# An index load moved behind the columns, and the first gate and up matmuls in a new order, in a kernel that TensorE bounds

## The chip, the cores and the metric

The kernel runs on one core of one Trainium2 chip. The metric is the device time of one execution in microseconds (us). Every run named here is "fast" (no more than 1.5% above the fastest run of its kernel). TensorE is the matmul engine, VectorE and ScalarE are the two elementwise engines, and a load is "landed" when its semaphore says so to the engine that waits.

In the profile lines PE is TensorE, PEld its weight loads, DVE VectorE, ACT ScalarE, POOL GpSimd, SP SyncE (which issues the loads here). L502 is line 502 of the kernel. Times in a view count from the start of the span, which is about 1.7 us shorter than the device time.

## The reference, cut to what matters

```python
def reference(A_x, A_w_r, A_w_i, B_x, B_w_gate, B_w_up, B_w_down):
    x = A_x                                   # (1, 2048, 512) bf16
    xn = _layernorm(x, axis=-1)
    # _A_ref: rfft2 of xn, times (w_r + 1j * w_i), irfft2
    # _B_ref: (gelu(xn @ w_gate) * (xn @ w_up)) @ w_down,  inner size 1792
    return x + _A_ref(xn, A_w_r, A_w_i) + _B_ref(xn, B_w_gate, B_w_up, B_w_down)
```

The change touches only the first microseconds of the second branch: the first rows of `xn`, and the first gate and up projections.

## The kernel before: the parts concerned

The rows are read in 16 "columns" of 128 rows (row 16p + c goes to partition p of column c). Columns 0 and 1 come first; then the index table for gathers much later; then the weights of the gate (`Wg_sb`) and of the up projection (`Wu_sb`), each in two halves: contraction blocks 0 and 1, then 2 and 3.

```python
    pin(load_x(0, 1))
    pin(load_x(1, 1))
    idx_t = pc.tile([P, 3], I32, name="idx_t")
    nc.sync.dma_start(out=idx_t[:], in_=nc.inline_tensor(idx_np, name="spec_rows").ap())
    for T in (Wg_sb, Wu_sb):
        for e in range(0, NE, 2):
            load_w(T, 0, 1024, e=slice(e, e + 2))     # a first or a second half
        if T is Wg_sb:
            load_x(2, 2)                              # columns 2 and 3
    # ... (cut: further columns, weights, constants)
```

The instruction streams of all engines come from a small planner. It is given operations with keys, assumed durations and assumed landing times, and writes down an order; the chip then runs each engine's stream in that order. Units 0 to 3 are the first four pieces of the projections: column 0 and then column 1, each with output blocks 0 to 3 and 4 to 7. Each unit takes 16 gate matmuls and 16 up matmuls of 128 columns, half of them on a first half of the weights.

```python
        T(0, 0)                                  # PE: transposes of column 0
        T(0, 1)
        add("PE", 0.28, spin_on, ...)            # 5 matmuls that only keep TensorE busy
        table = add("ACT", 1.3, lambda: None, [o["root", 1]], key=-1500, lat=1.3)
        # ... (cut)
        o["t", 0] = add("PE", 0.12, lambda: f_T(1, 0, 2), [o["xn1"]], key=1000.13, ...)   # transposes of column 1
        o["t", 1] = add("PE", 0.12, lambda: f_T(1, 2, 2), [o["xn1"]], key=1000.14, ...)
```

## Time and profile before

| before | |
|---|---|
| time, median of the first 3 runs | 178.68 us (178.48 to 178.89) |
| span of the profiled run | 176.9 us |
| TensorE busy | 171.2 us, 97% |
| first gate matmul begins | 6.45 us |
| first up matmul begins | 10.46 us |
| first gate matmul of 256 columns begins | 14.48 us |

The last three rows are moments of TensorE's timeline. They cut the head, that is all up to the first gate matmul of 256 columns, into stretches: what comes before the first useful matmul, the gate matmuls of units 0 to 3, and their up matmuls with the transposes of columns 2 and 3 among them.

### The profile page before, as it was taken

Reading aid. Unit: us, or ns where it says so; the run is one execution under the profiler, and the core shown is the slowest. Engines: PE = TensorE matmul, PEld = TensorE weight load, DVE = VectorE, ACT = ScalarE, POOL = GpSimd, SP = SyncE. Lnnn points to the kernel's source line nnn. Section 1 sums busy time; section 2 is a strip of 40 time slices with the busy share of each in tenths; the row PEclk is TensorE's granted clock in tenths of the full one; section 3 lists DMA queues with packets and bytes.
Section 4 is the critical chain, followed back from the end, with each engine's and each line's share of the span. In section 5 each row is a group of like instructions: output and inputs, shape, how many; then the busy total and the mean of one; then the engine's idle time right before and its main releaser. Section 6 shows DMA issues by size and latency. Waiting matters only on the chain.

```text
span 176.9 us, 3177 instructions
## 1 busy us (share of the span) xinstructions
PE 171.2 (97%) x1158; PEld 96.6 (55%) x1176; DVE 115.6 (65%) x255; ACT 96.4 (55%) x171; POOL 16.7 (9%) x38
## 2 busy tenths in 40 slices
PE   7799999999999999999999999999999999999993
PEld 7699845455545554555555454555445445444463
DVE  3568999988334499969899799843516325345333
ACT  4372489997734998889999973544112111211200
POOL 1020330407750000000000000000000000000000
PEclk9999999999999999999999999999999999999999
DMA  4999997264709602111112312010122222221212
GB/s 100 356 391 382 365 197 115 60 81 106 214 20 310 227 0 59 44 45 33 40 26 60 93 57 59 17 46 0 59 89 89 80 73 67 81 88 60 64 58 59
DMA packets 20847, 19.35 MB, mean 109 GB/s; under 512 B 8480, under 2 KB 17952, under 8 KB 20832
## 3 DMA queue, kind: packets, MB, share of 16 engines
q1 hardware_dynamic: 20416, 17.84, 35.8%
q0 software_dynamic: 416, 1.32, 2.6%
q8 instruction: 9, 0.15, 0.3%
q14 instruction: 6, 0.05, 0.1%
HBM read 13.38 MB, written 2.10 MB: 87 GB/s over the span
## 4 chain that ended last, share of the span: by engine, by line
PE 94%; DMA 2%; issue 1%; SPq 1%; DVE 0%
PE y_ps L833 27%; PE g_ps L494 25%; PE u_ps L494 25%; DMA Wg_sb<-in_B_w_gate_dram 2%; PE g_ps L502 2%; PE yp L784 2%; PE dp L651 2%; PE gp L754 2%; PE u_ps L502 2%; PE bp L593 2%; PE y_ps L837 2%; PE ep L660 2%; SPq L273 0%; PE tp L351 0%; SPq L284 0%
## 5 line engine op out<-in xcount | busy, mean ns | idle before, releaser
L494 PE MATMUL g_ps<-xnT,Wg_sb 128*128 128x512 bf16 (+1 forms) x220 | 52.8, 364 | 0.3
L494 PE MATMUL u_ps<-xnT,Wu_sb 128*128 128x512 bf16 (+1 forms) x216 | 52.5, 364 | 0.3
L833 PE MATMUL y_ps<-Wd_sb,hT 128*128 128x512 bf16 (+2 forms) x246 | 50.8, 355 | 0.3
L512 DVE TENSOR_TENSOR hT<-u_ps,ge 128x512 bf16<-128x512 f32 x56 | 38.4, 688 | 17.2 <-PE u_ps L494 12.4
L507 ACT ACTIVATE ge<-g_ps 128x512 bf16<-128x512 f32 x56 | 33.2, 599 | 21.9 <-PE g_ps L494 19.1
L833 PEld LDWEIGHTS <-hT 128*128 128x128 bf16 x252 | 23.2, 98 | 22.2
L494 PEld LDWEIGHTS <-Wg_sb 128*128 128x128 bf16 x224 | 21.5, 98 | 20.9
L494 PEld LDWEIGHTS <-Wu_sb 128*128 128x128 bf16 x224 | 21.4, 98 | 20.2
L790 ACT CAST yf<-yp 128x512 bf16<-128x512 f32 x16 | 9.3, 586 | 39.4 <-PE yp L784 39.4
L840 DVE TENSOR_TENSOR y_sb<-y_ps,y_sb 128x512 bf16<-128x512 f32 (+2 forms) x18 | 11.1, 631 | 27.9 <-PE y_ps L837 27.9
L665 ACT CAST E<-ep 64x512 bf16<-64x512 f32 x32 | 18.5, 579 | 2.0 <-PE ep L660 1.6
L339 DVE BATCH_NORM_STATS2 stats<-x_t 128x6 f32<-128x512 bf16 x16 | 10.4, 674 | 2.4 <-DMA x_t<-in_A_x_dram 2.4
L456 ACT ACTIVATE xn<-x_t,nb,rstd 128x512 bf16<-128x512 bf16 x12 | 9.4, 807 | 0.6 <-POOL nb L370 0.4
L563 ACT CAST Gs<-gp 128x512 bf16<-128x512 f32 x16 | 8.7, 592 | 1.0 <-PE gp L754 1.0
L563 ACT CAST ds<-dp 128x512 bf16<-128x512 f32 x16 | 8.9, 597 | 0.0
L796 DVE TENSOR_TENSOR lv<-yf 128x512 bf16<-128x512 bf16 x16 | 6.1, 422 | 4.1 <-ACT yf L790 3.2
L563 ACT CAST Bs<-bp 128x512 bf16<-128x512 f32 x16 | 8.3, 601 | 0.5 <-PE bp L593 0.5
L784 PEld LDWEIGHTS <-Gs 128*128 128x128 bf16 x64 | 4.8, 98 | 3.5
L803 DVE TENSOR_TENSOR yt<-lv 128x512 bf16<-128x512 bf16 x16 | 6.1, 422 | 0.3
L784 PE MATMUL yp<-CT,Gs 128*128 128x128 bf16 x64 | 6.0, 220 | 0.1
L837 PE MATMUL y_ps<-yt,RI_t 128*128 128x512 bf16 (+2 forms) x18 | 6.1, 356 | 0.0
L697 DVE TENSOR_TENSOR m<-X,TW 128x1024 bf16<-128x1024 bf16 x8 | 5.5, 688 | 0.2
(67 smaller groups left out, 130.6 us busy)
## 6 DMA issues: line engine op xcount, KB each, us to landing
F<-F SPq DMA_DIRECT2D x32, 64.0 KB, 2.0
y_sb<-in_A_x_dram SPq DMA_DIRECT2D x16, 128.0 KB, 2.1
out_dram<-y_sb SPq DMA_DIRECT2D x15, 128.0 KB, 1.7
x_t<-in_A_x_dram SPq DMA_DIRECT2D x7, 256.0 KB, 8.9
Wd_sb<-in_B_w_down_dram SPq DMA_DIRECT2D x1, 1792.0 KB, 7.5
Wg_sb<-in_B_w_gate_dram SPq DMA_DIRECT2D x2, 512.0 KB, 4.7
Wu_sb<-in_B_w_up_dram SPq DMA_DIRECT2D x2, 512.0 KB, 6.6
Wg_sb<-in_B_w_gate_dram SPq DMA_DIRECT2D x1, 768.0 KB, 9.8
```

The costliest lines, as they stand in the source:

```text
L339: V.bn_stats(out=st[:], in_=x_t[:, c, :])
L456: xn_op[c] = add("ACT", 0.72, lambda c=c: A.activation(out=xn[:, c, :], in_=x_t[:, c, :], func=AF.Identity, bias=nb[:, c:c + 1], scale=rst ...
L494: T_.matmul(b[name][:, f], lhsT=W_[:, e, (f0 + f) * P:(f0 + f + 1) * P], rhs=rhs[:, e, :], start=(e == 0), stop=(e == NE - 1))
L507: A.activation(out=b["ge"][:], in_=b["g_ps"][:], func=AF.Gelu_apprx_tanh)
L512: V.tensor_tensor(out=hT_of(sb, f0, m, o, w), in0=b["u_ps"][:], in1=b["ge"][:], op=ALU.mult)
L563: A.copy(out=o, in_=i)
L665: A.copy(out=b["E"][64 * h:64 * h + 64, r], in_=b["ep", h][64 * r:64 * r + 64])
L784: T_.matmul(t[:, q], lhsT=late["G"][:, q, c0 + j], rhs=IQ[q], start=(q == 0), stop=(q == 3), skip_group_check=True)
L790: A.copy(out=b["yf"][:, j], in_=b[j][:])
L833: T_.matmul(b[o][:], lhsT=hT_of(sb, f, 1, cl * P, P)[:, 0], rhs=Wd_sb[:, f, o:o + w], start=(f == 0), stop=False)
L837: T_.matmul(b[o][:], lhsT=late["RI"][:, c, :], rhs=late["yt"][:, c, o:o + w], start=False, stop=True)
L840: V.tensor_tensor(out=b["y"][:, o:o + w], in0=b[o][:], in1=b["y"][:, o:o + w], op=ALU.add)
```

## The change

Its intent: the weights' issue should follow column 1's at once; TensorE should have work that needs only first halves while second halves are under way, and column 1's transposes should stand early enough to allow that. The rest are new assumed times for the planner, and a small activation that pulls the load of the gelu table forward.

```diff
     pin(load_x(1, 1))
     idx_t = pc.tile([P, 3], I32, name="idx_t")
-    nc.sync.dma_start(out=idx_t[:], in_=nc.inline_tensor(idx_np, name="spec_rows").ap())
     ...
     load_x(14, 2)
+    nc.sync.dma_start(out=idx_t[:], in_=nc.inline_tensor(idx_np, name="spec_rows").ap())
     load_consts("F0", "L0")
     ...
-    LAND = {0: 2.7, 1: 3.4, 2: 7.2, 3: 7.2}
+    LAND = {0: 2.7, 1: 3.4, 2: 7.9, 3: 7.9}
-    WG_LAND = [6.6] * 8 + [13.2] * 6
+    WG_LAND = [7.35] * 8 + [13.2] * 6
     ...
-        table = add("ACT", 1.3, lambda: None, [o["root", 1]], key=-1500, lat=1.3)
+        table = add("ACT", 1.3, lambda: A.activation(out=warm[:], in_=eps_t[:], func=AF.Gelu_apprx_tanh), [o["root", 1]], key=-1500, lat=1.3)
     ...
-        o["t", 0] = add("PE", 0.12, lambda: f_T(1, 0, 2), [o["xn1"]], key=1000.13, lat=0.3, acq=("S",))
-        o["t", 1] = add("PE", 0.12, lambda: f_T(1, 2, 2), [o["xn1"]], key=1000.14, lat=0.3, acq=("S",),
+        o["t", 0] = add("PE", 0.12, lambda: f_T(1, 0, 2), [o["xn1"]], key=1000.01, lat=0.3, acq=("S",))
+        o["t", 1] = add("PE", 0.12, lambda: f_T(1, 2, 2), [o["xn1"]], key=1000.02, lat=0.3, acq=("S",),
     ...  (parts() takes one key for each half)
-            g = parts("g_ps", gt, Wg_sb, 1000 + 0.1 * (k % 2) + 0.4 * (k // 2), (5.3, WG_LAND[0]))
-            u = parts("u_ps", ut, Wu_sb, 1001 + 0.1 * (k % 2) + 0.4 * (k // 2), (8.6, WU_LAND[0]))
+            g = parts("g_ps", gt, Wg_sb, (1000 + (0, 0.03, 0.04, 0.05)[k], 1000.06 + 0.01 * k), (6.0, 7.8))
+            u = parts("u_ps", ut, Wu_sb, (1001 + 0.1 * k, 1001.4 + 0.1 * k), (9.5, 10.85))
```

More of the change, by code (lines that the diff above doesn't have):

```diff
@@ L524, in unit, with parts @@
         if k < 4:
-            def parts(name, tag, W_, key, t):
+            def parts(name, tag, W_, keys, t):
                 o = None
-                for e in (0, 2):
-                    o = add("PE", occ / 2, lambda e=e: mm_part(name, tag, W_, e), [o] if o else [], lat=occ / 2 + 0.3,
-                            key=key + 0.1 * e, acq=() if o else (tag,), t_min=t[e // 2])
-                    o.deps.append(xT_op[c0, 0] if e == 0 else xT_op[c0])
-                    if k == 1 and W_ is Wg_sb:
-                        between["t", 0].deps.append(o) if e == 0 else o.deps.append(between["t", 1])
+                for i, key in enumerate(keys):
+                    o = add("PE", occ / 2, lambda e=2 * i: mm_part(name, tag, W_, e), [o] if o else [], key=key,
+                            lat=occ / 2 + 0.3, acq=() if o else (tag,), t_min=t[i])
+                    o.deps.append(xT_op[c0] if i else xT_op[c0, 0])
+                    if W_ is Wg_sb and i == 0:
+                        if k == 0:
+                            between["t", 0].deps.append(o)
+                        else:
+                            o.deps.append(between["t", 1])
                 return o
             gt = ut = "GU"[k // 2]
-            g = parts("g_ps", gt, Wg_sb, 1000 + 0.1 * (k % 2) + 0.4 * (k // 2), (5.3, WG_LAND[0]))
-            u = parts("u_ps", ut, Wu_sb, 1001 + 0.1 * (k % 2) + 0.4 * (k // 2), (8.6, WU_LAND[0]))
+            g = parts("g_ps", gt, Wg_sb, (1000 + (0, 0.03, 0.04, 0.05)[k], 1000.06 + 0.01 * k), (6.0, 7.8))
+            u = parts("u_ps", ut, Wu_sb, (1001 + 0.1 * k, 1001.4 + 0.1 * k), (9.5, 10.85))
         else:
```

## The prediction

> **What bounds the kernel now.** I read five views in this order: the page (busy times and chain shares), the chain of work in order of time for the first 15 us, the waits of TensorE and of its weight loads, the head in slices of 0.1 us, and the timeline of the head. First the page.
>
> ```profile
> PE 171.2 (97%) x1158; PEld 96.6 (55%) x1176; DVE 115.6 (65%) x255; ACT 96.4 (55%) x171; POOL 16.7 (9%) x38
> ...
> PE 94%; DMA 2%; issue 1%; SPq 1%; DVE 0%
> ```
>
> TensorE is busy for 97% of the span and is 94% of the chain that ended last. The only transfer in that chain is a load of the gate weights, 2%. So there is hardly an engine to relieve: the time is the moment at which TensorE begins its real work, plus its matmuls, plus holes, plus the tail. The chain in order of time shows that moment (columns: start, length, what).
>
> ```profile
> 2.18 4.23 DMA Wg_sb<-in_B_w_gate_dram
> 6.41 0.05 issue
> 6.45 1.07 PE g_ps L502 x16
> 7.52 0.22 PE tp L351 x4
> 7.74 0.03 issue
> 7.77 2.85 PE g_ps L502 x48
> 10.63 1.34 PE u_ps L502 x24
> 11.97 0.45 PE tp L351 x8
> 12.41 2.23 PE u_ps L502 x40
> ```
>
> The first half of the first gate weights (contraction blocks 0 and 1 of four) is issued at 2.18 and lands at 6.41; TensorE starts at 6.45. After 16 matmuls and the 4 transposes of column 1 there is a second piece of "issue" at 7.74. The waits tell what that is (columns: total us, times, longest).
>
> ```profile
> PE sp_ps L320 <- DVE minus_half L266: 1.1, 1, 1.1
> PE g_ps L502 <- DMA Wg_sb<-in_B_w_gate_dram: 0.5, 1, 0.5
> PE tp L351 <- DVE xn L345: 0.4, 1, 0.4
> ...
> PEld L502 <- DMA Wg_sb<-in_B_w_gate_dram: 0.9, 2, 0.7
> ```
>
> These are all of TensorE's listed waits, in the whole run: 2.0 us, all before 6.5 us. Two belong to the gate weights. One is 0.5 us in front of the first matmul. The other shows only in the weight loads: 0.9 in two times, the longest 0.7, so 0.2 us is left for a second wait, and the timeline puts it before 7.77. That is the second half (blocks 2 and 3): issued at about 2.65, landed about 5.1 us later, at 7.74. From 7.77 on nothing is waited for.
>
> **Check of that reading.** Counting the code's matmuls after the first four transposes and the five spinning ones gives 426 of 128 columns, 79 of 256 and 625 of 512. At N/2.4 + 2.5 ns each (below) that is 23.78 + 8.62 + 134.90 = 167.3 us. From 6.45 that would end at 173.75; the last matmul of the chain ends at 174.15. Only 0.4 us is not matmul pitch, of which 0.2 is the wait just found and some 0.15 the drain of the last matmul. So a gain at the head passes to the end almost whole, unless it opens a new hole.
>
> **What the skill says.** (1) "TensorE: Matmul & The Clock Gate", section "Wait — 56ns, not 53.3ns?": a warm matmul of N columns follows the last after N/2.4 + about 2.5 ns. The trace agrees: 14 matmuls of 512 columns take 3.02 us in the chain, 0.216 each. (2) "Perfetto Trace Analysis", section "DMA Instruction — HWDGE (DVE, Sync)": the profiled slice of a DMA issue is the sequencer's use of the descriptor generator, not the data movement. The trace agrees: the index load's slice is 0.42 us, though its 1.5 KB land 2.0 us after issue, and the next issue starts only behind that slice. (3) "DMA: Bandwidth & Descriptors", section "Queues, rings and completion order": each DMA engine consumes its descriptors in ring order. So the tiny index load stands in front of the weights on all engines it uses; slices of the head agree (columns after the engines' busy times: clock, DMA share, GB/s):
>
> ```profile
> 2.30:2.40 0.10, 0.10 (x3) 0.10 (x2) 0.00 (x0) 0.09 (x1) 0.00 (x0) 1.00 1.27 359
> 3.30:3.40 0.10, 0.10 (x4) 0.10 (x3) 0.10 (x1) 0.00 (x0) 0.00 (x0) 1.00 1.96 123
> 3.60:3.70 0.10, 0.10 (x4) 0.10 (x3) 0.10 (x1) 0.00 (x0) 0.00 (x0) 1.00 0.44 41
> 4.20:4.30 0.10, 0.10 (x6) 0.10 (x4) 0.10 (x1) 0.09 (x1) 0.00 (x0) 1.00 1.16 410
> ```
>
> Columns 0 and 1 move up to 2.9 us, the index rows around 3.3 (queues full, few bytes), then near silence, and the weights stream at about 400 GB/s from 4.0 on. (4) "ScalarE: Activation LUTs", section "What ACT_TABLE_LOAD costs": about 1283 ns. The trace has 1.28 twice.
>
> **The change, part by part.**
>
> *Index load moved from third place to behind the columns.* It removes one 0.42 us issue slice; the first weight issue moves from 2.18 to 1.71, 0.47 us earlier. All later loads stand in the same order in one stream that runs at its limit, so they land about 0.45 earlier too: first half 6.41 to about 5.97, second half 7.74 to 7.3, columns 2 and 3 from 8.37 to 7.9, first up-projection half from about 9.9 to 9.4. The planner's new constants agree: it now assumes 6.0, 7.35, 7.9 and 9.5. I take 6.0 for TensorE's start. It can't be much before 5.77, when the spinning matmuls that begin at 5.49 run out (5 x 0.056), so at most 0.2 more is to be had. The table of rows is first used by the gathers at 41.0 us; it will land around 20. It takes over the place in the rotation of DMA semaphores that the first constants had; constants are needed only at some 55 us.
>
> *Order of the first 64 gate matmuls.* Before: 8 + 8 with the first half, 4 transposes, then at once the second half. After (from the instruction order of both kernels): 8, the 4 transposes, then 56 without a break, of which by the keys the first 24 use only first halves (units 1, 2, 3). Work that needs no second half is then 32 matmuls and 4 transposes, 36 x 0.056 = 2.0 us: the second half is wanted at 6.0 + 2.0 = 8.0, and is there at 7.3. The 0.2 us wait goes. What it asks for in return: unit 2 needs column 1's first copy. Transposes end at 6.0 + 12 x 0.056 = 6.67; in the trace the copy begins 0.31 behind the first transpose (7.36 to 7.67) and takes 0.29, then a 0.05 hop: 6.45 + 0.31 + 0.29 + 0.05 = 7.10. Unit 1's 8 matmuls keep TensorE to 6.67 + 0.45 = 7.12. Just enough; I allow 0.05 for it.
>
> *The gelu table loaded early.* Now it is loaded with a 0.3 us activation, behind the second square root, at 5.4, not at 8.17. These two lines of the timeline are what moves:
>
> ```profile
> 7.78 0.37 ACT L354 COPY xnT<-tp 128x256 bf16<-128x256 bf16 x1 [2.38 <-PE tp L351]
> 8.17 1.28 ACT L507 ACT_TABLE_LOAD   x1
> ```
>
> Table and activation end at about 5.4 + 1.28 + 0.3 = 7.0, so column 1's second copy may wait 0.1 to 0.2 and ends at 7.4. It is needed only by unit 2's second half, after 8.9. The four gelus, which began at 9.46 behind the table, can begin near 8.8. None of this is on the path; it only keeps PSUM free in time.
>
> *Order of the first 64 up-projection matmuls.* All first halves come before second ones. The trace shows no wait there now, so nothing is removed; with u starting near 9.85 and its first half landing at 9.45, the margin is 0.4. The normalisation of columns 2 and 3 ended at 11.78 just as their transposes began at 11.80; both move earlier, by 0.45 and 0.6, so up to 0.05 may appear.
>
> **Sum.** 0.45 (start) + 0.20 (second half) - 0.05 (copy, columns 2 and 3) = 0.60 us. 178.68 - 0.60 = 178.08, so 178.1 us: 0.3% faster.
>
> **Rivals.** (a) *A new wait eats it*: unit 2 waits for the copy longer than reckoned (the margin is nil), or column 3's transposes wait. For: both margins are under 0.1 us. Against: each can cost a few tenths only, and 0.45 remains. Time then 178.2 to 178.4. (b) *The index rows cost more than their issue slice*: the weights begin to flow 1.8 us behind their issue, column 0's bytes 1.15 (0.80 to 1.95). If the odd 0.6 is the index rows' doing, the weights land by 5.5, TensorE starts at 5.77, and the gain is 0.68 + 0.2: 177.8. Against: the silence at 3.6 to 4.0 lies behind the index rows, which looks like the latency of the weights' own issue; and the new constants say 6.0. (c) *The reshuffled plan opens a hole later*: the order of matmuls changes all the way to 116 us (forward transforms are moved by one unit; two units pair up). For: VectorE is 90% busy for long stretches. Against: the old plan, made by the same procedure, ran without a wait, and with two PSUM buffers of each kind one unit lasts 1.73 us against 0.69 on VectorE and 0.60 on ScalarE. Time then 178.4 to 179. (d) *Nothing moves*, the stream being the bound: 178.7. Against: it stands idle at 3.6 to 4.0, so an earlier issue starts it earlier.
>
> **Range and chances.** Centre 178.1. (b) sets the lower end, 177.75; (a), part of (c) and the spread of the runs of before (0.4 us between lowest and highest) the upper, 178.55. For 2% the time must move by 3.6 us, six times all head waits that the change can reach: faster 0.01, slower 0.01 (a bad stall in the new plan), same 0.98.
>
> **What would show it.** Right: the first weight issue at 1.7, its landing and the first gate matmul at 5.9 to 6.05; no wait of TensorE on gate weights beyond 0.1 in front of that matmul, and one place, not two, in the weight loads' waits; first up matmul near 9.85, first 256-column gate matmul near 13.9; span 176.3. Wrong: a first matmul still at 6.4; a wait of TensorE on the copies at 7.1 or on u's weights at 9.8; any wait behind 15 us. If the start comes before 5.85, rival (b) is right.

## The result

The changed kernel took 178.30 us, median of 4 runs (178.13 to 178.47); the kernel before took 178.73 in the same rounds (178.48 to 178.89). The ratio is 0.9977, 95% interval 0.996 to 0.9995. Ratios are the mean time of one kernel's fast runs over that of the other's of the same rounds, so not quite the ratio of the medians. The gain is 0.43 us by medians where 0.60 was predicted. The time lies inside the stated range.

Of the profile after, first the page's lines of busy time and of the shares of the chain that ended last.

```profile
PE 171.9 (97%) x1159; PEld 97.5 (55%) x1176; DVE 116.1 (66%) x255; ACT 96.2 (54%) x172; POOL 17.4 (10%) x38
...
PE 97%; issue 1%; DVE 0%
```

The load of the gate weights, 2% before, has left the chain, and TensorE's own pieces fill it from the start. The chain in order of time for the head (start, length, what):

```profile
5.66 0.53 PE sp_ps L324 x5
6.19 0.50 PE g_ps L502 x8
6.69 0.22 PE tp L351 x4
6.92 3.13 PE g_ps L502 x56
10.04 1.34 PE u_ps L502 x24
...
11.39 0.72 PE tp L351 x8
12.11 2.23 PE u_ps L502 x40
```

There is no load and no hole before the gate matmuls, and 56 of them run without a break. But two pieces are longer than their pitch: the 5 spinning matmuls (0.53 us, where 5 x 0.056 = 0.28) and the transposes of columns 2 and 3 (0.72 us, where before they took 0.45). The only wait of the weight loads that is left, beside the one for the first memset, belongs to these transposes:

```profile
PEld L351 <- DVE xn L345: 0.2, 1, 0.2
```

The timeline of VectorE shows what they wait for:

```profile
8.23 1.29 DVE L339 BATCH_NORM_STATS2 stats<-x_t 128x6 f32<-128x512 bf16 x2 [1.10 <-DMA x_t<-in_A_x_dram]
...
10.92 0.74 DVE L345 TENSOR_SCALAR xn<-x_t,mv,rstd 128x512 bf16<-128x512 bf16 x2 [1.18 <-POOL rstd L361]
```

Columns 2 and 3 are there at 8.2, column 3 is normalised at 11.66, and its first transpose starts at 11.71. The chain doesn't show this wait as one: it lies inside the piece of 8 transposes, 0.27 us of its 0.72. So "PE 97%" does not mean that TensorE's own work sets the time here. What does is worked out behind the experiments.

The three moments now stand at 5.99, 9.88 and 14.18 us in the timeline. So of the 14.48 - 14.18 = 0.30 us that this profile gains:

| stretch | before | after | gain |
|---|---|---|---|
| start of the first gate matmul | 6.45 | 5.99 | 0.46 |
| gate matmuls, 64 and 4 transposes | 4.01 | 3.89 | 0.12 |
| up matmuls, 64 and 8 transposes | 4.02 | 4.30 | -0.28 |

The second row holds the wait that went (0.2) less something that came (about 0.1). That something is the clock, which also lengthens the five spinning matmuls in front by 0.25. Stretches of half a microsecond, with the spinning matmuls alone, show it (stretch, its length, TensorE's busy time and count; then clock, DMA share, GB/s). One line of before, then two of after:

```profile
4.00:4.50 0.50, 0.50 (x12) 1.00 0.88 324
```

```profile
4.00:4.50 0.50, 0.50 (x8) 1.00 0.97 377
4.50:5.00 0.50, 0.50 (x7) 1.00 1.03 393
```

The count is of matmuls that run at any time in the stretch; it jumps to 12 where the clock is warm and stays at 7 or 8 where it is cold. The pitch is 0.53/5 = 0.106 us in the cold line of the chain above, against 0.056 warm. In the profile of before TensorE reached full speed at 4.0 us, by the trace's clock records, and in that of after at 6.2 us. The column of granted clock says 1.00 in both: it does not show this state, the pitch does. In the profile of before the warm clock came long before the first useful matmul; in that of after the first two gate matmuls still ran at half speed. The profile of before is also of one of that kernel's quicker runs (178.61 us), so the two profiles show less gain than the medians.

The gelu table did what was predicted. In the timeline of ScalarE after the change:

```profile
5.32 1.28 ACT L412 ACT_TABLE_LOAD   x1
...
8.74 2.06 ACT L507 ACTIVATE ge<-g_ps 128x512 bf16<-128x512 f32 x4 [1.41 <-PE g_ps L502]
```

The table is in at 6.6 us, and the gelus begin at 8.74 (9.46 before), behind their own gate sums.

### The profile page after: what moved, and what is told of

Same layout as the page of the kernel before. It is cut to its first block, busy times and chain, and to the rows that moved or that the text cites. A ratio compares the mean times of both kernels' runs of the same rounds, so it can differ in the third digit from the quotient of the medians.

```text
span 176.6 us, 3181 instructions
## 1 busy us (share of the span) xinstructions
PE 171.9 (97%) x1159; PEld 97.5 (55%) x1176; DVE 116.1 (66%) x255; ACT 96.2 (54%) x172; POOL 17.4 (10%) x38
## 4 chain that ended last, share of the span: by engine, by line
PE 97%; issue 1%; DVE 0%
PE y_ps L836 27%; PE g_ps L494 25%; PE u_ps L494 25%; PE sp_ps L320 2%; PE yp L787 2%; PE bp L596 2%; PE g_ps L502 2%; PE gp L757 2%; PE u_ps L502 2%; PE dp L654 2%; PE y_ps L840 2%; PE ep L663 2%; PE tp L351 1%; PE sp_ps L324 0%; DVE y_sb L843 0%
## 5 line engine op out<-in xcount | busy, mean ns | idle before, releaser
L663 PE MATMUL ep<-ds,CT 128*128 128x512 bf16 x16 | 5.7, 379 | 0.0
```

## Theories

**Theory A.** The change takes both waits for gate weights away and so moves the bound of the head from a load to TensorE's own stream. Part of the gain is lost again where loads behind the first weight half have not landed earlier by as much as their issue: the transposes of columns 2 and 3 wait for column 3.

**Theory B.** The first pair of profiles is not typical: TensorE's clock and the landings vary from run to run by as much as the gain, and a typical run gives the full 0.6 us.

A third possibility, that the reshuffled plan opens or closes something behind the head, could be settled without an experiment of its own. In all 14 profiles (of ten programs), I took the device time of the profiled run less the start of the first 256-column gate matmul: it lies between 164.12 and 164.14 us. Whatever a version gains or loses is therefore in the first 15 us, and each run's time tells its head.

## The experiments

All gave correct results. The first four shared one chip, the other eight another; the kernel before measured 178.82 us (mean of 10) on the one and 178.84 (mean of 12) on the other. In the first call one run of before took 180.48 us and was still counted as fast; it pulls the four ratios of that call down by some 0.0008, so I compare medians and means there. The stated means leave that run out. For e9 to e12 the ratios rest on runs that are mostly older; I compare versions with each other.

### e1: the changed kernel again

No edit.

> The changed kernel once more, unaltered, for a tighter interval and a second profile. Theory A (the small rest of the expected gain is lost at the transposes of columns 2 and 3, because the loads behind the first weight half land only some 0.15 us earlier): ratio 0.9970 to 0.9980 again (0.35 to 0.5 us), and TensorE's piece for these 8 transposes again takes 0.65 to 0.75 us where their pitch is 0.45. Theory B (the first profile was odd because TensorE's clock warmed only at 6 us, where in the kernel before it warmed at 4 us; a warm execution gives the full 0.6 us): the spinning matmuls are fast from 4 us on in this profile, the first gate matmul starts by 5.85, and the ratio is 0.9965 or lower.

Measured: 178.35 us (178.21 to 178.68, 6 runs), before 178.86; ratio 0.9967 (0.9935 to 0.9998). The transposes of columns 2 and 3 took 0.72 us again. The clock was warm at 5.5 us, the first gate matmul began at 6.00. The column 3 wait is thus no accident of one profile. The full 0.6 us did not come. For theory B this is no clean test: the clock was warm at 5.5 us and not at 4, and column 0 was 0.28 us later than in the first profile (its statistics began at 3.23, there at 2.95).

### e2: the index load alone

```diff
-    nc.sync.dma_start(out=idx_t[:], in_=...)      # third place
     ...
     load_x(14, 2)
+    nc.sync.dma_start(out=idx_t[:], in_=...)      # all else as in the kernel before
```

> The kernel before with only the index load moved behind the columns; the order on TensorE, VectorE and ScalarE is that of before. If the first half lands 0.5 to 0.8 us earlier but the second half only 0.15 (as in the changed kernel's profile), the first gate matmul starts near 5.9, 16 matmuls and 4 transposes are done by 7.1, and TensorE then waits about 0.5 us for the second half at 7.6: first up matmul at 10.2 to 10.3 where before had 10.46, gain only 0.15 to 0.25 us (ratio 0.9986 to 0.9992). If the whole stream moves up by 0.45 as the prediction had it, the gain is 0.45 us (ratio 0.9975).

Measured: 178.58 us (178.34 to 179.07), before 178.86; mean 178.64 against 178.82, so 0.18 us gained. The size fits the first expectation, but the profile does not show the reason given there: the first gate matmul began at 6.46, no earlier than before, because column 0 itself was late (its statistics began at 3.42 us, before: 3.05). The chain then ran through the second half of the up weights:

```profile
3.68 7.80 DMA Wu_sb<-in_B_w_up_dram
```

In this execution the earlier issue bought nothing: columns 2 and 3 came at 8.77 (before: 8.37), and the first 256-column gate matmul stood at 14.72, later than before. Its six runs spread from 178.34 to 179.07. That was the first sign of the late landings that e9 shows.

### e3: the orders and the table, without the index load's move

```diff
     idx_t = pc.tile([P, 3], I32, name="idx_t")
+    nc.sync.dma_start(out=idx_t[:], in_=...)      # back in third place, else the changed kernel
```

> The changed kernel with the index load back in third place: only the orders and the early gelu table are new. First gate matmul at 6.4 as before; the 0.2 us wait for the second half is gone: first up matmul at 10.25. Columns 2 and 3 arrive at 8.37 as before, so their transposes (normalised at 11.78) would begin at 11.6 and wait 0.1 to 0.2 us for column 3: gain at the end 0.05 to 0.2 us, ratio 0.9989 to 0.9997. If the two parts simply add (prediction), it is 0.2 us.

Measured: 178.52 us (178.22 to 178.86), mean 178.52 against 178.82: 0.30 us gained, more than the 0.05 to 0.2 expected. The profile does not contradict the expectation. It shows 0.14 us less than the profile of before (178.47 against 178.61), and by the expected way: columns 2 and 3 came at 8.39, and column 3's transposes waited. The mean gain is larger because the profile of before is of a quick run. What I had wrong is the start. The first half of the gate weights, issued at 2.18 as before, landed 3.9 us later and not 4.2. TensorE's timeline has the first gate matmul at 6.08:

```profile
6.08 0.62 PE L502 MATMUL g_ps<-xnT,Wg_sb 128*128 128x128 bf16 x8 [0.20 <-DMA Wg_sb<-in_B_w_gate_dram]
```

The earlier start was no gain in this profile. TensorE then waited for the first half of the up weights (landed 10.14, first up matmul 10.19) and for column 3.

### e4 and e10: the transposes of columns 2 and 3 one unit later

```diff
-            t = add("PE", 0.23, lambda c=c: f_T(c, 0, NE), [xn_op[c]], key=-880 + c, lat=0.5, acq=("S",))
+            t = add("PE", 0.23, lambda c=c: f_T(c, 0, NE), [xn_op[c]], key=1001.35 + 0.01 * c, lat=0.5, acq=("S",))
```

On TensorE only these 8 transposes move, behind 32 up matmuls and no longer behind 24.

> The changed kernel with the 8 transposes of columns 2 and 3 one unit (8 up matmuls, 0.45 us) later on TensorE; nothing else moves. Theory A: the wait for column 3 (0.2 to 0.3 us) is covered by these 8 matmuls and goes to the end: 0.2 to 0.3 us faster than the changed kernel, ratio to before 0.9960 to 0.9968, the transposes' piece back at 0.45 us. If the wait is not on the path or its place is taken by another (second half of the up weights, or the copies before the first 256-column gate matmul), it is equal to the changed kernel, 0.9977.

Measured: 178.21 us (177.88 to 178.46); mean 178.18, 0.21 us below e1's 178.39. The chain shows the wait gone:

```profile
10.30 1.79 PE u_ps L502 x32
12.08 0.45 PE tp L351 x8
12.53 1.79 PE u_ps L502 x32
```

> The version with the later transposes of columns 2 and 3 again. Theory A: 0.15 to 0.3 us faster than the changed kernel of this same call, and a narrower spread, since a late landing of these columns is covered by 8 more matmuls. Rival (the gap in the first call was chance): equal within 0.1.

The second time: 178.39 us (178.05 to 178.87), ratio 0.9972 (0.9956 to 0.9989), equal to the changed kernel (178.38). Three runs stood at 178.05 to 178.19 and three at 178.59 to 178.87. Over both calls the means are 178.29 (12 runs) for this version and 178.41 (15 runs, with the first four) for the changed kernel; their standard errors are 0.08 and 0.05. That the wait goes is shown by the trace; that it is worth 0.1 us on average is likely and not proved. The spread did not get narrower. In this version the spread comes from elsewhere: in e10's profile column 0 was late (3.40), TensorE began its gate matmuls at 6.44 and reached column 3's transposes 0.59 us after they were ready. That says nothing of the changed kernel itself (see below).

### e5 and e6: ten more spinning matmuls in front of the gate matmuls

```diff
     def spin_on():
-        for k in range(5):
+        for k in range(15):
```

> The kernel before with 15 instead of 5 matmuls that only keep TensorE busy in front of the first gate matmul (0.56 us more if the clock is warm, up to 1.07 if it is cold). Theory A (in the kernel before TensorE idles there for the weights, 0.5 us in its profile): at most 0.1 to 0.3 us slower, ratio 1.000 to 1.0015. Rival (TensorE, not the weights, sets the first gate matmul in most executions of the kernel before too): 0.5 us slower or more, ratio 1.003.

In the kernel before: 178.76 us (178.60 to 179.20), before 178.80; ratio 1.000 (0.9986 to 1.0013). The extra work costs nothing. Its profile shows why, and it's not only the wait for the first half: that had landed at 6.02, and the spinning matmuls held the first gate matmul back to 6.49. But the gate matmuls behind the transposes, which need the second half (landed 7.75), start at 7.80, where before they started at 7.77. So what set the head of the kernel before is the second half of the gate weights; a later start in front of it is absorbed. It is also the only wait for gate weights that is left among those of the weight loads:

```profile
PEld L502 <- DMA Wg_sb<-in_B_w_gate_dram: 0.2, 1, 0.2
```

> The changed kernel with the same 10 extra matmuls. Theory A (the change has moved the bound of the start from the weights to TensorE's own work in front of them, as three profiles without any wait for gate weights say): the whole extra work shows, up to what the wait for column 3 gives back (0.2 to 0.3): 0.3 to 0.6 us slower than the changed kernel, ratio to before 0.9990 to 1.0010. Rival (the weights still set the start): same as the changed kernel, 0.997 to 0.998.

In the changed kernel the same edit costs about 0.4 us: 178.79 us (178.44 to 179.07), ratio to before 0.9998 (0.9984 to 1.0012), where the changed kernel itself has 178.35 and 178.38. They were run at other times. The chain goes straight from the spinning matmuls to the gate:

```profile
5.66 0.84 PE sp_ps L324 x15
6.50 0.45 PE g_ps L502 x8
```

By the times, work that is free in the kernel before costs 0.4 us in the changed one, so the slack at its head is smaller than the 0.56 us that ten warm matmuls take. The trace doesn't show that TensorE's stream is the bound, though: in this profile too the transposes took 0.71 us, waiting for column 3 (columns 2 and 3 came at 8.48), and the later start was absorbed there. The first half of theory A is not shown by this pair.

### e7 and e11: without the early table load

```diff
-        table = add("ACT", 1.3, lambda: A.activation(out=warm[:], in_=eps_t[:], func=AF.Gelu_apprx_tanh), ...)
+        table = add("ACT", 1.3, lambda: None, ...)
```

> The changed kernel without the early activation, so that the gelu table is loaded behind column 1's copy as before. Expected: the table then loads at about 7.3 to 8.6 and the first gelu, which waits for its gate sums until 8.7 anyway, starts at 8.7 to 8.8 as in the changed kernel; time equal, ratio to the changed kernel's 1.000 within 0.0008. Rival (the early table is part of the gain): the first gelu later than 9.4, up-projection matmuls waiting for their PSUM buffer, 0.2 us slower or more.

> The changed kernel without the early table load again; the first time it was 0.3 us slower with a wide spread (178.25 to 179.1), though its profile shows no wait that goes back to the table, only a late landing of columns 2 and 3 (8.72). If that was chance: equal to the changed kernel of this call within 0.15 us. If the early table is worth something that the profile hides: 0.3 us slower again.

Measured: 178.69 us (178.25 to 179.10), ratio 0.9989 (0.9971 to 1.0006), and again 178.81 us (178.34 to 178.90), ratio 0.9993 (0.998 to 1.0007). I had expected it to equal the changed kernel. By medians it is 0.3 and 0.4 us slower than the changed kernel of the third call (178.38), by the means of all runs 0.27; within the third call alone the means differ by 0.16 (178.68 against 178.52), which is near their noise. No profile shows a way from the table to the end. The timeline of e7:

```profile
7.64 1.28 ACT L507 ACT_TABLE_LOAD   x1
9.04 2.06 ACT L507 ACTIVATE ge<-g_ps 128x512 bf16<-128x512 f32 x4
```

The gelus begin at 9.04, and the up matmuls, which need their buffers, began at 10.18 without a wait. What made e7's profiled run slow (178.82 us) stands in its chain, a late landing of columns 2 and 3 at 8.72:

```profile
2.69 6.03 DMA x_t<-in_A_x_dram
```

The profile of e11 fell in a quick run (178.39 us) and has the first 256-column gate matmul at 14.25, as the changed kernel. The 12 runs fall into two groups, five at 178.25 to 178.55 and seven at 178.81 to 179.10, so the version was more often in the slow group than the changed kernel (two of 15 runs above 178.7). Whether the table load does that or chance did, stays open.

### e8: later transposes, and no spinning matmuls

```diff
-        add("PE", 0.28, spin_on, [o["T", 0, 1]], key=-1500, lat=0.28, after=o["T", 0, 1])
     # (with the edit of e4)
```

> The later transposes of columns 2 and 3, and the 5 spinning matmuls taken out. Theory A: the first gate matmul starts at column 0's first copy, about 5.75, no longer at 6.0; gain over the version with later transposes 0.1 to 0.25 us, ratio to before 0.994 to 0.996. Rival (the clock warms later because TensorE idles up to 0.3 us before the copy, or the weights are not there at 5.75): equal or slower than the version with later transposes, 0.9953 or above.

Measured: 178.40 us (178.11 to 178.90), ratio 0.997 (0.9957 to 0.9982): no gain over e4 or e10. The profile fell in its slowest run, and it shows how late a landing can be. Its chain starts with the first half of the gate weights:

```profile
1.71 5.19 DMA Wg_sb<-in_B_w_gate_dram
```

Issued at 1.71, it landed at 6.90, and TensorE waited 1.0 us. This expectation of theory A failed: taking TensorE's work away in front of the gate does not help, since the load is then the bound again in at least some executions.

### e9: the changed kernel a third time

> The changed kernel a third time, to stand beside the three below on one chip. Expected ratio 0.9965 to 0.998. In the profile, if landing of columns 2 and 3 is what spreads the runs, the first 256-column gate matmul stands at 14.2 to 14.5 and the piece of 8 transposes at 0.65 to 0.75.

Measured: 178.38 us (178.28 to 178.82, 5 runs), ratio 0.9978 (0.9963 to 0.9993). Three runs stood at 178.28 to 178.38 and two at 178.80 and 178.82, as slow as the kernel before. The profile caught one of the slow ones. Its chain:

```profile
0.80 2.60 DMA x_t<-in_A_x_dram
...
5.41 0.72 PE tp L351 x4
6.13 0.53 PE sp_ps L324 x5
```

Column 0 landed 2.60 us after its issue, where it took 2.1 to 2.2 in the profiles of the result. What follows on TensorE shifts: its transposes begin at 5.41 and not 4.97, the first gate matmul at 6.45 in the timeline, though the first half of the weights had landed at 5.6. The first 256-column gate matmul stands at 14.66, beyond the 14.5 that I had expected at most. The chain leads back to column 0, but columns 2 and 3 came late too (8.72), and their transposes again waited (0.66 us). So here an earlier column 0 would only have made that wait longer.

I then put the start of column 0's statistics side by side for all 14 profiles, with the moment at which the first packet of 2048 bytes (that is, of the weights) starts, counted from the trace:

```
                         first weight packet    column 0's statistics begin
index load third (4):    3.25 to 3.28           3.00 3.05 3.06 3.08
index load last (10):    2.79 to 2.84           2.95 2.96 3.06 3.08 3.08 3.20 3.23 3.40 3.42 3.42
```

With the index rows in third place column 0 is always there by 3.1. With the weights directly behind column 1, their packets start before column 0 is signalled as landed, and in half of the profiles column 0 is 0.1 to 0.4 us late. The packets of the two columns tell the same: the last of the 256 ends at 3.08 to 3.25 us in the four, and at 3.10 to 3.60 in the ten. That the two go together is measured; that the weights' packets cause it, by sharing the engines with the columns' last packets, is an argument.

### e12: later transposes, index load in third place

```diff
     idx_t = pc.tile([P, 3], I32, name="idx_t")
+    nc.sync.dma_start(out=idx_t[:], in_=...)      # third place, with the edit of e4
```

> The version with later transposes, but with the index load back in third place: what the index load's move alone is worth once nothing else waits. The first gate matmul then stands at the landing of the first half, 6.1 to 6.45, not at 6.0: 0.1 to 0.4 us slower than the version with later transposes. If the index load doesn't matter at all: equal within 0.1.

Measured: 178.37 us (178.14 to 178.61, 5 runs), ratio 0.9974 (0.996 to 0.9988), against 178.39 for e10 in the same rounds: equal. The first gate matmul stood at 6.35, the weights having landed at 6.3, and the means differ by no more than their noise. Three pairs differ in the index load alone, and the move gains by their means 0.17 us (e2 and before), 0.11 (changed kernel and e3) and 0.09 (e4 with e10, and e12), each about as large as its own standard error of 0.1. So it is worth about 0.1 us, if anything, and not 0.45. That a late column 0 takes back what an earlier issue gives would explain this, but isn't shown.

### The versions side by side

| version | runs | mean us | gain |
|---|---|---|---|
| before | 26 | 178.81 | |
| index load alone (e2) | 6 | 178.64 | 0.17 |
| orders and table alone (e3) | 6 | 178.52 | 0.29 |
| before, 15 spinning matmuls (e5) | 6 | 178.82 | -0.01 |
| changed, 15 spinning matmuls (e6) | 6 | 178.77 | 0.04 |
| changed, without the table (e7, e11) | 12 | 178.68 | 0.13 |
| changed kernel (result, e1, e9) | 15 | 178.41 | 0.40 |
| later transposes (e4, e10) | 12 | 178.29 | 0.52 |
| later transposes, index third (e12) | 5 | 178.38 | 0.43 |
| later transposes, no spinning five (e8) | 6 | 178.41 | 0.40 |

A mean of 5 or 6 runs has a standard error of about 0.1 us, one of 12 or more 0.04 to 0.08. Later transposes have the lowest mean of all; I would keep that edit, with the reservation stated at e10.

What sets the end of the head can be read from the traces, moment against moment. In eight profiles the transposes of column 3 had to wait for its normalisation:

| profile | first gate matmul | statistics of columns 2 and 3 begin | column 3 normalised | first gate matmul of 256 columns | device time |
|---|---|---|---|---|---|
| result | 5.99 | 8.23 | 11.66 | 14.18 | 178.31 |
| e1 | 6.00 | 8.31 | 11.73 | 14.26 | 178.38 |
| e11 | 6.30 | 8.31 | 11.73 | 14.25 | 178.39 |
| e3 | 6.08 | 8.39 | 11.81 | 14.34 | 178.47 |
| e6 | 6.34 | 8.48 | 11.90 | 14.42 | 178.56 |
| e9 | 6.45 | 8.72 | 12.14 | 14.66 | 178.80 |
| e7 | 6.11 | 8.74 | 12.16 | 14.69 | 178.82 |
| e2 | 6.46 | 8.77 | 12.19 | 14.72 | 178.85 |

In all eight the first transpose of column 3 starts 0.06 us behind its normalisation, the first 256-column gate matmul 2.52 or 2.53 us behind it, and the device time is the start of the statistics plus 170.08 us within 0.01. The first gate matmul moves by half a microsecond between them, the clock is warm in some and cold in others, and neither shows in the time. So in the changed kernel it is the landing of columns 2 and 3, with the 3.4 us of normalisation behind it, that sets the end of the head. Seven of the eight have the changed order; in e2, with the old order, the wait was only 0.04 us, just behind the up weights.

In the other six profiles TensorE came to column 3's transposes after they were ready: by 0.24 and 0.26 us in the two of the old order (before, e5), where the second half of the gate weights had held it, and by 0.25 to 0.59 us in the four with later transposes (e4, e8, e10, e12). In those four, the start of TensorE's gate matmuls and its clock behind it set the time. That also explains why e4's edit pays in some executions and not in others: it gains only where columns 2 and 3 are late against TensorE. All this is of profiled executions; that the others follow the same is likely and not shown.

## Why the prediction was right, point by point

**Bound and direction: right.** TensorE bounds the kernel and only the head can move. The time behind the head is the same within 0.02 us in all 14 profiles, which also refutes rival (c), a new hole later.

**The start, 0.45 us: the number was right in the first profile, by luck.** The weight issue moved to 1.71 as predicted, and the first gate matmul moved from 6.45 to 5.99, so 0.46. But the reason was another. The prediction let TensorE start when the first half lands, at 5.97; the half landed at 5.57, and TensorE's own spinning matmuls, at the cold pitch, filled the time to 5.99. Also, the 6.41 that the step starts from was a late landing: the other three profiles with the index load third have the first half there 3.8, 3.9 and 4.1 us after 2.18, so at 6.0 (e5 and e3) and 6.3 (e12). And column 0, which had been given no part in the sum, is late by up to 0.4 us in half of the ten profiles in which the weights follow at once.

**"All later loads [...] land about 0.45 earlier too": the step that failed.** Columns 2 and 3 were to come at 7.9; in the result's profile they came at 8.23, 0.14 us earlier than before (8.37). By the sum found above, 7.9 would have given an estimated 7.9 + 170.08 = 177.98 us, if nothing else had bound then; 8.23 gives the measured 178.31. Without its wait of 0.27 us for column 3, that profile would stand at 178.04, beside the 178.08 predicted: this step accounts for what it lacks. Means over the four profiles with the index load third and the ten with it last, whose issue was 0.47 us earlier:

| what | index load third (4) | last (10) | earlier by |
|---|---|---|---|
| first gate half landed | 6.19 | 5.89 | 0.30 |
| second gate half landed | 7.72 | 7.53 | 0.19 |
| statistics of columns 2 and 3 begin | 8.36 | 8.53 | -0.18 |
| first up half landed | 9.99 | 9.90 | 0.09 |

The bulk of the stream did come earlier: in the result's profile the 512th of the packets of 2048 bytes ended at 6.42 us, before at 6.70. But the landings of whole loads did not keep that lead, and for columns 2 and 3 they scatter, between 8.23 and 8.85 in the ten against 8.27 to 8.39 in the four. Why is open. Likewise, the margin of 0.4 us that the prediction gave to the first up half was 0.16 in the result's profile (9.72 and 9.88).

**The second half's wait, 0.2 us: right.** No profile of the new order has it; before and e5 both do. It counted for more than the sum says: it, and not the start, set the head of the kernel before (e5).

**The copy and columns 2 and 3, -0.05: the mis-sized term.** The copies cost nothing. The transposes of columns 2 and 3 cost 0.27 us in the first profile and in e1 (0.72 against 0.45), because TensorE came 0.6 us earlier and the columns only 0.14. This was rival (a), and it came true. What it said against itself, that such a wait costs a few tenths and leaves 0.45, does not hold: a wait for column 3 fixes the end whatever the start, and in the profiled runs of e9 and e7 (178.80 and 178.82) nothing was left. e4 takes the wait away in the trace.

**The gelu table, nothing on the path: open.** The profiles agree with it: in e7 and e11, as in the result, columns 2 and 3 set the time. The times of the two, on average, do not quite.

**Rival (b)** is half right. The first half did land at about 5.5 (5.51 to 5.74 in six of the ten profiles with the index load last), but TensorE was not there by 5.77 to use it. Its reason is not shown: the silence before the weights stream is there without the index rows too, at 3.1 to 3.4 us. The prediction also misread its slice of 3.3 to 3.4 us. The trace has the 128 packets of the index rows between 2.79 and 3.30, at 9 ns each; what fills the queues at 3.3 are the first packets of the weights (2048 bytes, some 0.5 us each there, where later ones take 0.084). **Rival (d)** is refuted by the gain, though a part of it lives on in the landings that hardly moved.

**What was not in the prediction at all** is the clock. I took the warm pitch from 5.5 us on, from one profile. In the other 12 profiles that have the record TensorE became warm between 4.2 and 6.9 us. With the kernel before that hardly matters, as it idles until about 6; with the new order the chains give 0.50 us (result), 0.58 (e9) and 0.74 (e4) for the first 8 gate matmuls, where their warm pitch gives 0.45. In e4 this goes to the end; in the result and e9 it vanished in the wait for column 3. No run changed the 37 spinning matmuls at the kernel's start, which take 4.13 us at the cold pitch and stand directly before column 0's transposes in the chains of the result, e4 and e12.

Theory A is right that column 3's wait eats the rest of the gain. It is wrong that the bound moved to TensorE's own stream: in the profiles of the changed kernel it moved to another load, and only with later transposes is it TensorE's start. Theory B is right that landings and clock vary, and wrong that a typical run gives the full 0.6 us.

## What to carry to other kernels

When the wait of the bounding engine at the head is taken away, look at once for what stands next behind it. Here an earlier start of TensorE ended in the wait for columns 2 and 3, and a gain of 0.6 us became 0.4. A chain of 97% TensorE can hide such a wait: look for pieces that are longer than their pitch. To find what sets the time, compare moments over several profiles: the one that keeps a constant distance to the end (here 170.08 us in eight profiles) is the bound. A load that is issued earlier need not land earlier by as much; read the landing of each load that something waits for, before and behind the one that is moved. And for differences below 0.5%, one profile of each version is one draw: read landings and warm-up from several before building a sum on them.

## What the Trainium skill lacked or had wrong

- "TensorE: Matmul & The Clock Gate", section "What you observe", puts the change to the warm clock around 4 us into sustained matmuls, ±500 ns run to run. Here the first matmul starts at 1.05 us and the warm clock came at 4.0 to 6.9 us, 2.9 to 5.8 us behind it, over 13 profiles. The next section asks for a busy window of about 3.4 us; the 2.9 us of the earliest profile lie below that, and the whole range is far wider than ±500 ns.
- "DMA: Bandwidth & Descriptors", section "Anatomy of one DMA — SWDGE (gpsimd) path", gives a fixed cost of about 2.0 us, nearly constant, for loads that GpSimd issues; no page has such a fit for loads that SyncE issues. Here, on SyncE's path, the 128 KB of column 0 landed 2.1 to 2.6 us after issue, and the 512 KB of the first weight half, behind other loads, 3.8 to 5.2.
- No page has a figure for how much of an earlier issue reaches the landings of the loads behind it: 0.47 us at the issue became 0.30, 0.19 and 0.09 us for three weight loads on average, and nothing for columns 2 and 3. Nor does one say how much later a load lands when the next stands closer behind it (column 0's statistics began at 2.95 to 3.42 us against 3.00 to 3.08); that the closeness is the cause is not shown here.
- No page treats the column of granted clock in the profile view used here. It reads 1.00 also before the trace's first clock record (4.0 to 6.9 us), where matmuls of 128 columns follow each other at 0.106 us; the pitch and the record itself tell.
